# Attention and two gated layers: where conversions and projection groups stand around the ends of the attention chunks

## The chip, the cores and the metric

The kernel runs on one core of one Trainium2 chip. The metric is the device time of one execution in microseconds (us); less is better. Three executions of the kernel before took 965.5, 968.14 and 969.22 us, with a median of 968.14 us.

## What is computed

A causal attention with a window of 128 and a distance bias, then a gated layer (SiLU), then a second layer (Mish). Four sequences of 576 positions, eight heads of 64; its 2304 rows of 512 are the tokens of the two layers. Matrices arrive as 64-bit floats.

```python
# attention, per batch and head
scores = scale * np.matmul(q, k.transpose(0, 1, 3, 2))
mask = (rel >= 0) & (rel < window)
scores = np.where(mask, scores + bias[None], -1000000000.0)
attn = np.exp(scores - np.max(scores, axis=-1, keepdims=True))
attn = attn / (np.sum(attn, axis=-1, keepdims=True) + 1e-09)
out = np.matmul(attn, v)
...
# layer one, w_gate and w_val 512 x 1536, w_out 1536 x 512
g = x @ w_gate
silu = g * (1.0 / (1.0 + np.exp(-g)))
val = x @ w_val
x = silu * val @ w_out
...
# layer two, w_in 512 x 2048, w_out 2048 x 512
h = x @ w_in
sp = np.log1p(np.exp(h))
y = (h * np.tanh(sp)) @ w_out
```

## The kernel before

Numbers are kept as a high and a low part, and a product of two such numbers is three matmuls: high by high, high by low, low by high. `hi_act` makes the high part on ScalarE (line 121), `lo_dve` the low part on VectorE (line 124).

The 2304 tokens go in five chunks of 512, 384, 512, 512 and 384 (`A_CHUNKS`). Per chunk and head, the attention has these pieces. `score` multiplies on TensorE into a bank `s_ps`; VectorE adds bias and takes the maximum (line 233), ScalarE takes the exponential (line 237). `norm` takes a reciprocal on VectorE (line 248) and scales the probabilities on ScalarE (line 252) and, in chunk 0, partly on VectorE (line 254). `transp` transposes them on TensorE into `t_ps` (line 259), copies the bank to `PT` on ScalarE (line 265) and masks it twice on GpSimd (lines 268 and 272). `outp`, once for two heads, is the value product on TensorE into `o_ps`, whose high and low part become one quarter of `xt`, the input of layer one. Eight heads make four pairs and four quarters, 0 to 3.

Layer one of a chunk is a list of groups. For each of 12 columns of weights, `gv_groups` gives a gate group and a value group of 12 matmuls into `g_ps`, followed by ScalarE's tanh (line 628), VectorE's products (lines 629 and 637) and the parts `hh` and `hl`. `out_group` gives 12 matmuls of the output projection into four banks `acc0` to `acc3`. With a lag of one, the last output group of a chunk is carried into the next chunk's list. While a chunk's groups run, the next chunk's attention pieces are put between them: each piece has a cost, and is emitted when its share of the costs falls to the share of the groups that are done.

Weights are converted from 64-bit words on chip by `convert`: one pass on ScalarE (line 416, output `cg`) and four on VectorE (lines 428, 433, 421 and 439, outputs `cw` and `cp`), then `hi_act` and `lo_dve` into a tile `w` (layer one's gate and value weights, `conv_w1`) or `ring` (its output weights, `conv_ring`). The raw words come by DMA into `wst` and `wraw`, and the converted `ring` weights are also written to DRAM (`w1od`) for later chunks. All these steps wait in a queue `bg`, from which `pump` takes them. For the first attention `w` 0 and 1 and `ring` 0 are converted; the later ones are pumped during the groups of chunk 0. `begin` multiplies the first two columns by the quarters 0 and 1 of `xt`, and later by quarter 2, before the first attention is done.

The order of TensorE is that of the program (`manual_schedule`). The other engines' order is made by a scheduler with a timeline of its own, which may put a conversion ahead of attention work that comes earlier in the program. Each engine then works through its own order. DMAs are issued from the SP queue.

The main loop's emission of groups:

```python
for gi, (kind, i, f) in enumerate(groups):
    if ci == 0 and kind == "gv" and gi % 3 == 0:
        if i == 0:
            conv_ring(1)
        if i + 2 < NF1:
            conv_w1(i + 2)
    f()
    ...
    while win and (spent * ng < (gi + 1) * total or gi == len(groups) - 1):
        _, cost, e = win.popleft()
        e()
```

Of the kernel before, what the change touches and what calls it, by code (L numbers as in the profile page):

```python
# [18 lines left out]
B, H, S, D = 4, 8, 576, 64  # L19
# [3 lines left out]
NF1, NF2 = F1 // 128, F2 // 128  # L23
# [69 lines left out]
def body(ctx: ExitStack, tc: tile.TileContext, qT, kT, vP, w1, w1o, w2, cst, yT):  # L93
    nc = tc.nc
# [28 lines left out]
    def lo_dve(out, in_, hi):  # L123
        return nc.vector.tensor_tensor(out=out, in0=in_, in1=hi.bitcast(F32), op=ALU.subtract)  # L124
# [10 lines left out]
    def attention(ap, p, ci, s_native, upfront):  # L135
# [120 lines left out]
        def transp(h):  # L256
            t_ps = rot("t_ps")
            for q in sorted(p.qb, key=lambda q: -q.qn):
                nc.tensor.transpose(t_ps[:, q.c:q.c + q.qn], P_[h, q.idx][:q.qn], ident[:q.qn, :q.qn])  # L259
            pt = ap.tile([128, 2 * nb_, 128], F32, tag="PT", name="PT")  # L260
            pairs = pt.rearrange("p (u k) c -> p u k c", k=2)
            for u, m, n in p.runs:
                c = p.qb[u].c
                prev, here = pairs[:, u:u + m, 0, :n], pairs[:, u:u + m, 1, :n]
                nc.scalar.activation(  # L265
                    out=prev, in_=t_ps[:, c:c + m * n].rearrange("p (u c) -> p u c", u=m), func=AF.Copy
                )
                nc.gpsimd.affine_select(  # L268
                    out=here, in_=prev, pattern=[[0, m], [1, n]], compare_op=ALU.is_ge, fill=0.0,
                    base=0, channel_multiplier=-1,  # L270
                )
                nc.gpsimd.affine_select(
                    out=prev, in_=prev, pattern=[[0, m], [-1, n]], compare_op=ALU.is_gt, fill=0.0,
                    base=0, channel_multiplier=1,
                )
            pt_[h] = pt.rearrange("p s c -> p (s c)")

        def outp(pr):
            v = raw.pop(("v", pr))
            xt = x_t[ci]  # L280
            n = p.n
            o_ps = rot("o_ps")
            for i, x in enumerate(p.o_order):
                q, here = x.uses[0]
                c0, b0 = q.c, 256 * q.idx + 128 * here
                for e in range(2):
                    mm(
                        o_ps[64 * e:64 * e + 64, c0:c0 + x.w], v[:, x.vi, 64 * e:64 * e + 64],
                        pt_[2 * pr + e][:, b0:b0 + x.w], i == 0, False,
                    )  # L290
            hi_act(xt[:, 0, pr, :n], o_ps[:, :n])
            lo_dve(xt[:, 1, pr, :n], o_ps[:, :n], xt[:, 0, pr, :n])

        return SimpleNamespace(
            ci=ci, load=load, load_v=load_v, split=split, score=score, norm=norm, transp=transp,
            outp=outp, upfront=upfront, ns=len(p.sb), s_full=s_full, nk=len(p.kb),
        )

    early = {}

    def attention_pieces(atts):

# [55 lines left out]

        def t_piece(k):
            a, h = heads[k]  # L360
            return (a.ci, 0.48, lambda: a.transp(h))

        def delay(k):
            return CFG["delay0"] if heads[k][0].ci == 0 else 1
# [25 lines left out]
    def pump(n):  # L390
        while n > 0 and bg:
            k, f = bg.popleft()
            f()
            n -= 1
            if k is not None:
                done.add(k)
# [530 lines left out]
    with tc.manual_schedule(engines={mybir.EngineType.PE}):  # L927
# [28 lines left out]
        while at < lasts[0]:  # L956
# [10 lines left out]
            while bg and nst - len(bg) < f * nst:  # L967
                pump(1)
        carry = []
        for ci, p in enumerate(plansA):  # L970
            if ci < last:
                win = [pieces.popleft() for _ in range(lasts[ci + 1] - at)]
                at = lasts[ci + 1]
            else:
                pump(10000)
                att.__exit__(None, None, None)
                cv = tc.tile_pool(name="cv", bufs=2, side="right", reuse_waits="tile")
                bpool["p"] = cv.__enter__()
                win = []
                for b in range(NJ, NF2):  # L980
                    combos(b)
# [5 lines left out]
            if ci == last:  # L987
                first["x"] = load_x(xp, 0)
            groups = []
            outs = carry + [out_group(ci, i)[0] for i in range(NF1)]  # L990
            for i in range(NF1):
                groups += [("gv", i, f) for f in gv_groups(ci, i)]
                if i < len(carry) or len(outs) > NF1 - 1 - i + lag:
                    groups.append(("o", 0, outs.pop(0)))
            if ci == 0:
                groups[4:6] = groups[5], groups[4]
# [4 lines left out]
            win = collections.deque(win)  # L1001
            for gi, (kind, i, f) in enumerate(groups):
                if ci == 0 and kind == "gv" and gi % 3 == 0:
                    if i == 0:
                        conv_ring(1)
                    if i + 2 < NF1:
                        conv_w1(i + 2)
                f()
                if ci or not win:
                    pump(CFG["pump_g"])  # L1010
                elif gi % 3 == 0:
                    due = max(1, -(-len(bg) // 4))
                if not ci:
                    pump(due)
                while win and (spent * ng < (gi + 1) * total or gi == len(groups) - 1):
                    _, cost, e = win.popleft()
                    e()
                    spent += cost
                    pump(CFG["pump_p"] if ci else due)
# [76 lines left out]
```

## Time and profile before

| what | value |
|---|---|
| median of three executions | 968.14 us |
| the profiled execution | 969.0 us |
| its span, first to last instruction | 967.2 us |
| mean clock granted to TensorE | 0.994 of full |
| TensorE matmul busy | 924.9 us (96%) |
| TensorE weight loads busy | 828.4 us (86%) |
| VectorE busy | 701.2 us (72%) |
| ScalarE busy | 524.7 us (54%) |
| GpSimd busy | 193.8 us (20%) |

The page gives busy times over the whole span. A timeline row gives the start of an instruction (or of several alike), its duration, the engine, the line, what it writes and reads, and in brackets for how long the engine was idle before it and whose work ended that. In a row of a window, each engine's busy time is followed by its number of instructions, and PEclk is the clock granted to TensorE, 1.00 being 2.4 GHz and 0.50 being 1.2 GHz.

### The profile page before, as it was taken

To read this page: it belongs to the slowest core of one execution; us is meant where nothing else is said; L and a number is where in the kernel's file an instruction comes from. 1 tells how busy PE (TensorE), PEld (TensorE's weight loads), DVE (VectorE), ACT (ScalarE), POOL (GpSimd) and SP (SyncE) were. 2 spreads that over 40 slices of the span, in tenths; PEclk is the share of its full clock that TensorE was granted. 3 is DMA by queue.
4 is the path that set the end of the run, shared out by engine and by line. 5 is a ranking of instruction groups with operands and counts; after the bars stand their busy time and mean duration, and the time that the engine had idled before them with its cause. 6 is when DMAs were issued, how large, how long until landed. Compare 5 with 4: busy or idle time off the path is not lost.

```text
span 967.2 us, 14606 instructions
## 1 busy us (share of the span) xinstructions
PE 924.9 (96%) x5040; PEld 828.4 (86%) x5040; DVE 701.2 (72%) x1341; ACT 524.7 (54%) x1135; POOL 193.8 (20%) x332
## 2 busy tenths in 40 slices
PE   6879999999999999999999998799999999999998
PEld 4646777899988888887878998799999999999997
DVE  6989897688667865478434768778876888777673
ACT  6846666666666674455433445564544645455442
POOL 0321232111110222001103334442012320122000
PEclk9979999999999999999999999999999999999999
DMA  8865325386546733176306993624783257930375
GB/s 293 293 231 184 126 70 182 101 253 217 160 128 207 261 111 112 31 245 225 130 1 205 380 342 112 234 66 163 255 301 131 66 186 245 314 111 16 98 264 183
DMA packets 76921, 174.86 MB, mean 181 GB/s; under 512 B 9136, under 2 KB 52528, under 8 KB 67120
## 3 DMA queue, kind: packets, MB, share of 16 engines
q1 hardware_dynamic: 76848, 173.94, 54.0%
q8 instruction: 40, 0.66, 0.3%
q14 instruction: 33, 0.27, 0.1%
HBM read 138.25 MB, written 35.65 MB: 180 GB/s over the span
## 4 chain that ended last, share of the span: by engine, by line
PE 70%; DVE 10%; DMA 9%; ACT 4%; issue 3%; POOL 2%; SPq 2%; DVEq 0%; ACTq 0%; POOLq 0%
PE bk L114 29%; PE g_ps L114 24%; PE acc L114 11%; DMA wraw<-w 3%; PE s_ps L114 3%; PE o_ps L114 2%; DVE G L694 1%; DVE win L124 1%; POOL t L790 1%; DMA q<-qT 1%; PE t_ps L259 1%; DVE cw L433 1%; SPq L176 1%; DVE u L694 1%; DMA wout<-w2o 1%
## 5 line engine op out<-in xcount | busy, mean ns | idle before, releaser
L114 PE MATMUL g_ps<-xt,w 128*128 128x512 f32 (+1 forms) x1440 | 319.8, 375 | 5.1 <-DVE xt L124 3.8
L114 PEld LDWEIGHTS g_ps<-xt,w 128*128 128x128 f32 x1440 | 259.2, 189 | 42.5 <-DVE xt L124 5.0
L114 PE MATMUL bk<-xs,win 128*128 128x384 f32 x1008 | 179.1, 336 | 8.6 <-DVE G L694 6.0
L114 PEld LDWEIGHTS bk<-xs,win 128*128 128x128 f32 x1008 | 174.5, 188 | 12.7 <-DVE G L694 9.2
L114 PE MATMUL bk<-op,wout 128*128 128x384 f32 x1008 | 176.1, 334 | 1.7 <-DMA wout<-w2o 1.1
L114 PEld LDWEIGHTS bk<-op,wout 128*128 128x128 f32 x1008 | 174.7, 188 | 2.7 <-issue 1.8
L114 PE MATMUL acc<-hh,ring 128*128 128x512 f32 (+1 forms) x480 | 149.0, 373 | 1.7 <-DVE ring L124 1.7
L121 ACT ACTIVATE op<-G 128x768 fp32r<-128x768 f32 x84 | 70.8, 847 | 65.6 <-PE bk L114 63.1
L114 PEld LDWEIGHTS acc<-hh,ring 128*128 128x128 f32 x480 | 89.0, 188 | 14.6 <-DVE ring L124 2.3
L124 DVE TENSOR_TENSOR op<-G,op 128x768 fp32r<-128x768 f32 x84 | 80.3, 963 | 28.1 <-ACT op L121 27.4
L268 POOL TENSOR_SCALAR_AFFINE_SELECT PT<-PT 128x256 f32<-128x256 f32 (+4 forms) x80 | 44.5, 570 | 251.2 <-ACT PT L265 251.0
L114 PE MATMUL acc<-hl,ring 128*128 128x512 f32 (+1 forms) x240 | 88.6, 369 | 0.0
L790 POOL TENSOR_TENSOR t<-w 128x256 f32<-128x256 f32 x48 | 41.8, 891 | 230.3 <-DVE win L124 213.6
L237 ACT ACTIVATE Pt<-Pt,sm 128x128 f32<-128x128 f32 (+1 forms) x160 | 62.7, 395 | 16.2 <-DVE sm L233 15.5
L628 ACT ACTIVATE t<-g_ps 128x512 f32<-128x512 f32 (+1 forms) x60 | 32.9, 548 | 57.5 <-PE g_ps L114 57.4
L629 DVE SCALAR_TENSOR_TENSOR t<-t,g_ps 128x512 f32<-128x512 f32 (+1 forms) x60 | 37.7, 628 | 36.1 <-ACT t L628 36.0
L1040 ACT ACTIVATE G<-G 128x384 f32<-128x384 f32 x72 | 37.0, 521 | 49.2 <-DVE G L694 49.2
L694 DVE TENSOR_TENSOR G<-u,bk 128x384 f32<-128x384 f32 x72 | 39.0, 553 | 32.5 <-PE bk L114 30.3
L637 DVE SCALAR_TENSOR_TENSOR t<-t,g_ps 128x512 f32<-128x512 f32 (+1 forms) x60 | 37.9, 632 | 28.0 <-PE g_ps L114 26.7
L252 ACT ACTIVATE Pt<-Pt,sm 128x128 f32<-128x128 f32 (+1 forms) x144 | 46.5, 393 | 12.9 <-DVE sm L248 12.8
L121 ACT ACTIVATE hh<-t 128x512 fp32r<-128x512 f32 (+1 forms) x60 | 35.1, 585 | 32.9 <-DVE t L637 32.6
L124 DVE TENSOR_TENSOR hl<-t,hh 128x512 fp32r<-128x512 f32 (+1 forms) x60 | 40.6, 676 | 16.3 <-ACT hh L121 15.8
(78 smaller groups left out, 1240.5 us busy)
## 6 DMA issues: line engine op xcount, KB each, us to landing
wout<-w2o SPq DMA_DIRECT2D x42, 1024.0 KB, 6.3
wraw<-w SPq DMA_DIRECT2D x16, 1024.0 KB, 5.9
w2o<-chl SPq DMA_DIRECT2D x16, 896.0 KB, 8.9
wst<-w SPq DMA_DIRECT2D x12, 1024.0 KB, 7.9
cw<-w1od SPq DMA_DIRECT2D x24, 512.0 KB, 3.9
w<-w2d SPq DMA_DIRECT2D x24, 512.0 KB, 3.3
w2d<-cw SPq DMA_DIRECT2D x16, 512.0 KB, 4.6
wraw<-w1o SPq DMA_DIRECT2D x6, 1024.0 KB, 6.1
```

Of the source, the lines that this page charges most:

```text
L114: nc.tensor.matmul(out=out, lhsT=lhsT, rhs=rhs, start=start, stop=stop, skip_group_check=True)
L121: return nc.scalar.activation(out=out, in_=in_, func=AF.Copy)
L124: return nc.vector.tensor_tensor(out=out, in0=in_, in1=hi.bitcast(F32), op=ALU.subtract)
L237: nc.scalar.activation(out=Pt[:q.qn], in_=Pt[:q.qn], func=AF.Exp, scale=-1.0, bias=sm[:q.qn, i:i + 1], accum_out=sm[:q.qn, 8 + i:9 + i],)
L252: nc.scalar.activation(out=pt, in_=pt, func=AF.Copy, scale=r)
L268: nc.gpsimd.affine_select(out=here, in_=prev, pattern=[[0, m], [1, n]], compare_op=ALU.is_ge, fill=0.0, base=0, channel_multiplier=-1,)
L628: tanhs.append(nc.scalar.activation(out=t[:, :n], in_=st["g"][:, :n], func=AF.Tanh, scale=0.5))
L629: nc.vector.scalar_tensor_tensor(out=t[:, :n], in0=t[:, :n], scalar=1.0, in1=st["g"][:, :n], op0=ALU.add, op1=ALU.mult)
L637: nc.vector.scalar_tensor_tensor(out=t[:, :n], in0=t[:, :n], scalar=0.5, in1=vps[:, :n], op0=ALU.mult, op1=ALU.mult)
L694: nc.vector.tensor_tensor(out=out, in0=a, in1=b, op=op)
L790: nc.gpsimd.tensor_tensor(out=x[:, o], in0=a, in1=b, op=ALU.subtract)
L1040: nc.scalar.activation(out=out, in_=in_, func=AF.Mish)
```

## The change

Three things. First, while the groups of chunk 0 are emitted, each conversion step that `pump` takes is traced inside `issue_after`, which orders its instructions, on ScalarE behind the last copy to `PT` of the first attention, and on VectorE behind the low part of quarter 2 of `xt`; from chunk 1 on there is no such edge. Second, the cost of the last head's transposition is set from 0.48 to 3.08, and the output group that is carried over a chunk boundary goes to the head of the next chunk's list instead of behind its first two groups. Third, the first `conv_w1` in the loop goes ahead of `conv_ring(1)`.

```diff
--- before.py
+++ after.py
@@ -262,7 +262,7 @@
             for u, m, n in p.runs:
                 c = p.qb[u].c
                 prev, here = pairs[:, u:u + m, 0, :n], pairs[:, u:u + m, 1, :n]
-                nc.scalar.activation(
+                last_of["act"] = nc.scalar.activation(
                     out=prev, in_=t_ps[:, c:c + m * n].rearrange("p (u c) -> p u c", u=m), func=AF.Copy
                 )
                 nc.gpsimd.affine_select(
@@ -289,7 +289,7 @@
                         pt_[2 * pr + e][:, b0:b0 + x.w], i == 0, False,
                     )
             hi_act(xt[:, 0, pr, :n], o_ps[:, :n])
-            lo_dve(xt[:, 1, pr, :n], o_ps[:, :n], xt[:, 0, pr, :n])
+            last_of["x", pr] = lo_dve(xt[:, 1, pr, :n], o_ps[:, :n], xt[:, 0, pr, :n])
 
         return SimpleNamespace(
             ci=ci, load=load, load_v=load_v, split=split, score=score, norm=norm, transp=transp,
@@ -297,6 +297,8 @@
         )
 
     early = {}
+    last_of = {}
+    behind = []
 
     def attention_pieces(atts):
 
@@ -358,7 +360,7 @@
 
         def t_piece(k):
             a, h = heads[k]
-            return (a.ci, 0.48, lambda: a.transp(h))
+            return (a.ci, 0.48 + (2.6 if h == H - 1 else 0.0), lambda: a.transp(h))
 
         def delay(k):
             return CFG["delay0"] if heads[k][0].ci == 0 else 1
@@ -390,7 +392,10 @@
     def pump(n):
         while n > 0 and bg:
             k, f = bg.popleft()
-            f()
+            with ExitStack() as es:
+                for x in behind:
+                    es.enter_context(tc.issue_after(x.ins))
+                f()
             n -= 1
             if k is not None:
                 done.add(k)
@@ -967,7 +972,10 @@
             while bg and nst - len(bg) < f * nst:
                 pump(1)
         carry = []
+        behind += [last_of["act"], last_of["x", 2]]
         for ci, p in enumerate(plansA):
+            if ci:
+                behind.clear()
             if ci < last:
                 win = [pieces.popleft() for _ in range(lasts[ci + 1] - at)]
                 at = lasts[ci + 1]
@@ -987,10 +995,11 @@
             if ci == last:
                 first["x"] = load_x(xp, 0)
             groups = []
-            outs = carry + [out_group(ci, i)[0] for i in range(NF1)]
+            outs = [out_group(ci, i)[0] for i in range(NF1)]
+            groups += [("o", 0, f) for f in carry]
             for i in range(NF1):
                 groups += [("gv", i, f) for f in gv_groups(ci, i)]
-                if i < len(carry) or len(outs) > NF1 - 1 - i + lag:
+                if len(outs) > NF1 - 1 - i + lag:
                     groups.append(("o", 0, outs.pop(0)))
             if ci == 0:
                 groups[4:6] = groups[5], groups[4]
@@ -1001,10 +1010,10 @@
             win = collections.deque(win)
             for gi, (kind, i, f) in enumerate(groups):
                 if ci == 0 and kind == "gv" and gi % 3 == 0:
+                    if i + 2 < NF1:
+                        conv_w1(i + 2)
                     if i == 0:
                         conv_ring(1)
-                    if i + 2 < NF1:
-                        conv_w1(i + 2)
                 f()
                 if ci or not win:
                     pump(CFG["pump_g"])
```

What the scheduler and the program make of it, at three places. In these rows an `x3` counts rows alike, and the line numbers of the changed kernel are a few higher (428 is 433 there, 433 is 438, 421 is 426, 439 is 444, 629 is 634).

VectorE at the end of the first attention. Before, from the five passes ahead of quarter 2 of `xt` to quarter 3:

```order
L124 TENSOR_TENSOR w<-cw,w 128x1024
L428 TENSOR_SCALAR cw<-wst 128x1024 x2
L433 SCALAR_TENSOR_TENSOR cw<-wst,cw 128x1024 x2
L124 TENSOR_TENSOR xt<-o_ps,xt 128x512
L439 SCALAR_TENSOR_TENSOR cw<-cw,cp 128x1024
L421 TENSOR_SCALAR cp<-cg 128x512
L439 SCALAR_TENSOR_TENSOR cw<-cw,cp 128x1024
L124 TENSOR_TENSOR w<-cw,w 128x1024
L421 TENSOR_SCALAR cp<-cg 128x512
L428 TENSOR_SCALAR cw<-wraw 128x1024
L124 TENSOR_TENSOR w<-cw,w 128x1024
L124 TENSOR_TENSOR xt<-o_ps,xt 128x512
```

The same place in the change, from the last head's sums to quarter 3:

```order
L245 TENSOR_SCALAR sm<-sm 128x4
L248 RECIPROCAL sm<-sm 128x4
L254 TENSOR_SCALAR Pt<-Pt,sm 128x128 x2
L124 TENSOR_TENSOR xt<-o_ps,xt 128x512
L433 TENSOR_SCALAR cw<-wst 128x1024
L433 TENSOR_SCALAR cw<-wraw 128x1024
L438 SCALAR_TENSOR_TENSOR cw<-wst,cw 128x1024
L426 TENSOR_SCALAR cp<-cg 128x512
L438 SCALAR_TENSOR_TENSOR cw<-wraw,cw 128x1024
L444 SCALAR_TENSOR_TENSOR cw<-cw,cp 128x1024
L426 TENSOR_SCALAR cp<-cg 128x512
L124 TENSOR_TENSOR xt<-o_ps,xt 128x512
```

Before, five conversion passes stand ahead of quarter 2 of `xt`, and seven between it and quarter 3. In the change the sums, the reciprocal and the scaling of the last head are followed by quarter 2 at once, and the conversions begin behind it.

TensorE at the first transposition of chunk 1 (128x128 and 128x64, head 0). Before:

```order
L114 MATMUL acc_720<-hh,ring 128x512
L114 MATMUL acc_721<-hh,ring 128x512
L114 MATMUL acc_721<-hl,ring 128x512
L114 MATMUL acc_721<-hh,ring 128x512
L114 MATMUL g_ps<-xt,w 128x512 x12
L259 MATMUL t_ps<-cst_sb,Pt 128x128 x2
L259 MATMUL t_ps<-cst_sb,Pt 128x64 x2
L114 MATMUL s_ps<-k_634,q_633 128x256
```

In the change:

```order
L114 MATMUL acc_717<-hh,ring 128x512
L114 MATMUL acc_718<-hh,ring 128x512
L114 MATMUL acc_718<-hl,ring 128x512
L114 MATMUL acc_718<-hh,ring 128x512
L259 MATMUL t_ps<-cst_sb,Pt 128x128 x2
L259 MATMUL t_ps<-cst_sb,Pt 128x64 x2
L114 MATMUL g_ps<-xt,w 128x512 x12
L114 MATMUL s_ps<-k_634,q_633 128x256
```

The transposition has moved ahead of the 12 matmuls of a value group (`g_ps`), and stands directly behind an output group.

TensorE at the end of the last attention, that of chunk 4, during the groups of chunk 3. Before:

```order
L114 MATMUL acc_4614<-hl,ring 128x512
L114 MATMUL acc_4614<-hh,ring 128x512
L259 MATMUL t_ps<-cst_sb,Pt 128x128 x3
L114 MATMUL o_ps<-PT,v 64x256 x2
L114 MATMUL o_ps<-PT,v 64x128 x4
L114 MATMUL o_ps<-PT,v 64x256 x2
L114 MATMUL g_ps<-xt,w 128x512 x24
```

In the change the last two transpositions come first:

```order
L114 MATMUL g_ps<-xt,w 128x512 x12
L259 MATMUL t_ps<-cst_sb,Pt 128x128 x3
L114 MATMUL g_ps<-xt,w 128x512 x12
L259 MATMUL t_ps<-cst_sb,Pt 128x128 x3
L114 MATMUL acc_4611<-hh,ring 128x512
L114 MATMUL acc_4611<-hl,ring 128x512
```

and, after further groups of both kinds, the last value product:

```order
L114 MATMUL acc_4614<-hl,ring 128x512
L114 MATMUL acc_4614<-hh,ring 128x512
L114 MATMUL g_ps<-xt,w 128x512 x12
L114 MATMUL o_ps<-PT,v 64x256 x2
L114 MATMUL o_ps<-PT,v 64x128 x4
L114 MATMUL o_ps<-PT,v 64x256 x2
L114 MATMUL g_ps<-xt,w 128x512 x12
```

Before, the value product (`o_ps`) directly follows the last transposition. In the change three gate or value groups of 12 and two output groups stand between them, and one more gate or value group follows the value product.

## Rows read from the trace of the kernel before

**Rows 1.** The page's slices: clock granted to TensorE, tenths, 40 slices.

```profile
PEclk9979999999999999999999999999999999999999
```

**Rows 2.** Timeline, TensorE, 39 to 67 (start us, us, engine line op, idle before <- releaser).

```profile
39.06 1.81 PE L114 MATMUL s_ps<-qkv 64*128 64x256 f32 x8
...
42.06 0.66 PE L259 MATMUL t_ps<-cst_sb,Pt 128*128 128x128 f32 x4 [1.18 <-ACT PT L265]
...
44.44 4.85 PE L114 MATMUL g_ps<-xt,w 128*128 128x512 f32 x20 [0.79 <-DVE xt L124]
...
49.22 1.74 PE L114 MATMUL o_ps<-PT,qkv 128*64 128x256 f32 x16
...
50.89 0.81 PE L259 MATMUL t_ps<-cst_sb,Pt 128*128 128x128 f32 x4
...
54.78 1.19 PE L259 MATMUL t_ps<-cst_sb,Pt 128*128 128x128 f32 x4 [3.09 <-ACT Pt L252]
...
59.18 5.06 PE L114 MATMUL g_ps<-xt,w 128*128 128x512 f32 x11 [2.77 <-DVE xt L124]
...
64.17 1.92 PE L114 MATMUL o_ps<-PT,qkv 128*64 128x256 f32 x16
...
66.79 0.49 PE L114 MATMUL g_ps<-xt,w 128*128 128x512 f32 x1 [0.70 <-ACT xt L121]
```

**Rows 3.** Timeline, ScalarE, at 53.

```profile
53.33 1.11 ACT L416 ACTIVATE cg<-wraw 128x1024 bf16<-128x1024 bf16 x1 [2.23 <-DMA wraw<-w1o]
```

**Rows 4.** Timeline, VectorE, 54 to 67.

```profile
54.52 1.29 DVE L428 TENSOR_SCALAR cw<-wst 128x1024 int32<-128x1024 int32 x2 [2.75 <-DMA w1od<-cw]
...
58.45 0.68 DVE L124 TENSOR_TENSOR xt<-o_ps,xt 128x512 fp32r<-128x512 f32 x1
...
66.77 0.69 DVE L124 TENSOR_TENSOR xt<-o_ps,xt 128x512 fp32r<-128x512 f32 x1 [0.84 <-ACT xt L121]
```

**Rows 5.** Windows of 1 us (window, then us, busy and count per engine, PEclk, DMA).

```profile
54.00:55.00 1.00, 0.22 (x1) 0.18 (x1) 0.48 (x1) 1.00 (x4) 0.00 (x0) 0.68 1.04 442
...
64.00:65.00 1.00, 1.00 (x7) 0.58 (x8) 1.00 (x3) 0.00 (x0) 0.00 (x0) 0.70 0.00 0
```

**Rows 6.** Timeline, TensorE and VectorE, 80 to 85.

```profile
80.57 2.91 PE L114 MATMUL g_ps<-xt,w 128*128 128x512 f32 x12
...
84.41 0.89 PE L259 MATMUL t_ps<-cst_sb,Pt 128*128 128x128 f32 x4 [0.94 <-ACT Pt L252]
...
82.39 0.16 DVE L248 RECIPROCAL sm<-sm 128x4 f32<-128x4 f32 x1
```

**Rows 7.** Windows, two long stretches.

```profile
67.50:162.00 94.50, 91.53 (x451) 68.83 (x452) 87.29 (x199) 61.01 (x163) 21.57 (x43) 1.00 0.43 140
...
10.00:50.00 40.00, 35.18 (x146) 25.47 (x144) 39.62 (x136) 34.35 (x101) 11.23 (x18) 1.00 0.87 301
```

**Rows 8.** Timeline, GpSimd, masks of PT.

```profile
34.13 0.64 POOL L268 TENSOR_SCALAR_AFFINE_SELECT PT<-PT 128x512 f32<-128x512 f32 x1 [0.77 <-ACT PT L265]
...
58.98 2.21 POOL L272 TENSOR_SCALAR_AFFINE_SELECT PT<-PT 128x512 f32<-128x512 f32 x2
```

**Rows 9.** Timeline, TensorE, 505 to 511.

```profile
505.64 0.49 PE L259 MATMUL t_ps<-cst_sb,Pt 128*128 128x128 f32 x3
...
509.18 1.51 PE L114 MATMUL o_ps<-PT,v 128*64 128x256 f32 x14 [2.48 <-POOL PT L272]
```

**Rows 10.** Groups of instructions by line, VectorE conversion passes (count | busy, mean ns).

```profile
L439 DVE SCALAR_TENSOR_TENSOR cw<-cw,cp 128x1024 f32<-128x1024 f32 x34 | 42.5, 1249 | 0.2
...
L421 DVE TENSOR_SCALAR cp<-cg 128x512 int32<-128x512 int32 x34 | 15.2, 448 | 8.6 <-ACT cg L416 8.5
...
L428 DVE TENSOR_SCALAR cw<-wraw 128x1024 int32<-128x1024 int32 x22 | 15.8, 718 | 11.8 <-DMA wraw<-w 5.6 <-DMA x2d<-ev 2.7 <-DMA v<-vP 2.6
```

**Rows 11.** Timeline, VectorE, 182 to 184.

```profile
182.51 0.69 DVE L637 SCALAR_TENSOR_TENSOR t<-t,g_ps 128x512 f32<-128x512 f32 x1 [0.48 <-PE g_ps L114]
...
183.97 0.69 DVE L124 TENSOR_TENSOR hl<-t,hh 128x512 fp32r<-128x512 f32 x1 [0.77 <-ACT hh L121]
```

## The prediction

> **What bounds the kernel now.** I read the slices of the page first: the clock row of TensorE, which is busy for 96% of the span, has one dent, the third slice, from 48 to 73 us [rows 1]. The reader should see that this is the only place before the second layer where much time is lost. The TensorE timeline then names the losses in order [rows 2]. Head 6's transposition stands at 50.89; head 7's waits 3.09 us for ScalarE's normalisation; the matmuls on the third pair of attention outputs wait 2.77 us for VectorE's `xt`; after the last value product come 0.70 us. The queues of the other two engines say why. ScalarE stood 2.23 us at a conversion's first pass, `cg<-wraw`, whose DMA had not landed, with head 7's normalisation behind it [rows 3]. VectorE stood 2.75 us at a conversion that waited for a spill, and ran four conversion passes ahead of `xt` at 58.45 [rows 4]. The clock went to half during the first wait (0.68 in the microsecond from 54, 0.70 in that from 64 on its way back) [rows 5]: eleven matmuls took 5.06 us there, and twelve of the same kind take 2.91 at full clock [rows 2, 6]. From then on VectorE is the engine with least room: it is busy 87.29 of the 94.5 us from 67.5 to 162, and 39.62 of 40 in the stretch ahead [rows 7].
>
> **Part one: the tail of the first attention.** Twenty-one conversion passes that stood on VectorE between 37 us and the last `xt` become seven, and those stand behind the third `xt`; on ScalarE the passes go behind the last copy to `PT`. So nothing of a conversion can block the tail. I time the tail anew from 39.06, with the durations of before. Scores end at 40.87; the next transposition no longer waits 1.18 us for a `PT` copy that a conversion held up, nor the 24 matmuls behind it 0.79 [rows 2]: 49.22 becomes 47.3. Value product 1.67 (49.22 to 50.89) gives 49.0; two transpositions of some 0.7 give 50.4, as head 7's normalisation has no conversion in front. Twelve matmuls of 0.25 follow (20 took 4.85), to 53.4. GpSimd's masks are next: in the trace they end at 61.19, 5.22 us after head 7's transposition ended at 55.97 [rows 2, 8], so here at 55.6; TensorE waits 2.2 us. Value product 1.92 gives 57.5. From its end to the end of the last `xt` took 1.37 (66.09 to 67.46) [rows 2, 4], so 58.9 against 67.46: **8.6 us ahead**. Bounds: 10.8, if each mask takes the 0.64 of the row at 34.13 and not the 1.1 of those at 58.98 [rows 8], for TensorE then waits for nothing; 6.6 if the 2.0 us before 49.22 are not had.
>
> **What is late next.** The changed order puts head 0's transposition of the second chunk one group of twelve matmuls (2.91 us) earlier on TensorE, while on VectorE the reciprocal that it needs has two more 1.25 us passes (a `ring` and a `w`) between it and the last `xt`. Before, that reciprocal came 14.9 us after `xt` (82.39 less 67.46) [rows 4, 6]; with 2.3 more it comes at 58.9 + 17.2 = 76.1. The transposition followed 2.0 us later; the exponentials of head 1 that stood between are done by then, so I take 1.0: 77.1. TensorE would arrive at 83.47 - 67.46 - 2.9 after `xt`, that is 72.0, and waits 5.1 us where it waited 0.94 [rows 6]. Transposition and the twelve matmuls behind it end at 77.1 + 0.9 + 2.9 = 80.9; the same work was done at 85.3. So 4.4 of the 8.6 stay, **minus 4.2**. Bounds: nothing lost, if the passes fit into gaps; 6.2, if the 2.0 stays and the spill of the ring is waited for again.
>
> The clock is the next price. A wait of 3.09 us let it fall [rows 2, 5]; one of 2.48 us near 507 did not, since the slices there show 9 [rows 1, 9]. A wait of 5.1 is on the far side of the first. At half clock twelve matmuls cost about 2.6 more (5.06 for eleven against 2.91). While TensorE is slow VectorE works off its passes, which it would have had to be waited for anyway, so I take half, **minus 1.3**, between 0 (the row at 507) and 2.6. The Trainium skill (TensorE: Matmul & The Clock Gate, HAM oscillation — how this bites in real kernels) says that a wait in the middle of a kernel puts the array back to its low clock, so that what follows each one starts slow; by it this term is the full 2.6 and the forecast 1.3 later, and the trace agrees at 54 us but not at 507.
>
> Then the backlog. To the tenth product of a tanh with its gate, eleven more conversion passes stand behind the last `xt` than did: six long ones near 1.25, three of 0.45, two of 0.72 [rows 10], together 9.4 us when the 0.08 by which rows overlap is taken off. VectorE thus has 87.3 + 9.4, some 97 us of work from 58.9 on, where it got to 162 before. At a density of 0.97 that is 158.9, 3.1 us ahead; this is what the three terms leave (8.6 - 4.2 - 1.3), so they need 0.97, less than the 0.99 before 50 us and more than the 0.924 after it [rows 7]. I count nothing more for it, and keep 0.924 (163.9, 1.9 behind) for the range. The loads that move with the conversions are hidden: the SP queue holds the same ones, later, and their readers are later by as much.
>
> **Part two: the chunk boundaries.** Before the last chunk the last transposition (505.64) stands directly ahead of the last value product, which waits 2.48 us for its mask [rows 9]. The changed order has three groups of twelve gate or value matmuls and two of the output projection between them, far over the 2.5: **plus 2.5**. The other three boundaries have other heads' scores there and no such wait. The output projection that was carried into the next chunk now follows the one before it directly, so its operands, `hh` and `hl`, have to be ready in 2.8 us instead of after two groups more. At 182.51 the chain from VectorE's product to the end of `hl` takes 2.15 us [rows 11], so it mostly fits; I put **minus 0.4** for four boundaries, between 0 and 2. The swap of the first two conversions goes together with part one. The second layer's order on TensorE is unchanged, and costs nothing.
>
> **Sum:** 8.6 - 4.2 - 1.3 + 2.5 - 0.4 = 5.2. The profiled execution took 969.0, so 963.8; the median of the three runs lies 0.9 lower, and on its scale I forecast **962.9**.
>
> **Rivals.** *The tail's gain is kept*: masks run unblocked (10.8) and the clock stays: 10.8 - 4.2 + 2.5 - 0.0 = 9.1, or 959.0 on the median's scale; with the transposition's wait half gone, 957. For it speaks that a mask took 0.64 in places; against it that conversions now start just when the masks run.
>
> *All of the tail's gain is given back*: the wait at the transposition is the full 6.2 and the clock costs 2.6, so that only 2.1 from the boundaries is left: 966. This is also the case that part one does not do what it says, the wait only moving from one transposition to another.
>
> *Slower*: VectorE's backlog becomes the bound of the whole first chunk. The place is its queue from 58.9 to the tenth group, the price 97 us over its density. Below 0.922 the loss there passes the 2.1 of the boundaries, and the kernel is slower than before; at 0.86 the queue gets there at 171.7, 9.7 late, and the time is 975.7. For it: VectorE takes its order as it stands, whatever DMA or ScalarE pass it waits for, as at 54.52 [rows 4], and it showed 0.924 in this stretch [rows 7]; against: it had TensorE to wait for there, and 0.99 when it had work. The Trainium skill (Perfetto Trace Analysis, Identifying the Most-Contended Engine) takes the engine with the highest occupancy for the one to relieve and warns that a busy TensorE row is no measure; by it VectorE decides in this chunk, as in this rival, while the trace shows TensorE without waits there.
>
> **How the numbers follow.** The forecast case has 0.50, with 960 to 966 as its own range; the kept gain 0.22, the gain given back 0.18, the backlog 0.10. A measurement of this kernel can tell about 0.5% from no change, that is 963.3 and 973.0. A little over half of the forecast case (0.27) lies below 963.3, with all of the kept gain: faster 0.49. The rest of it (0.23), the given-back case and the mild end of the backlog (0.03): same 0.44. Slower 0.07. The range from 956 to 970 takes in the bounds of the terms and leaves out about 1 in 10 at either end.
>
> **What would show it.** Right: both waits of 3.09 and 2.77 gone, no DMA wait on ScalarE or VectorE between 50 and 56, the last `xt` of the first chunk done near 59; a wait of 4 to 6 us at the first transposition after it, perhaps with the clock at half; VectorE near 0.97 from 59 to 159; no mask wait near 505. Wrong: a last `xt` after 62, a new wait for `hl` over half a microsecond at the boundaries, or new TensorE waits in the second layer.

## The result and the profile after

The changed kernel takes 979.66 us in the median (four runs, 977.14 to 981.91) where the kernel before, run beside it, takes 968.68: 1.0126 of its time, 95% interval 1.0089 to 1.0163. It is about 11 to 12 us slower; faster was forecast. The profiled execution took 978.84 us, its span is 977.1, and TensorE's mean clock 0.991 of full. Of the executions behind the numbers below, two (one of the kernel before, 1028.64 us, and one with the carried group first, 1289.37 us) ran at a clock of 0.85 and 0.66; they stand in no ratio and move no median by more than 0.3 us.

The clock row of the page, against [rows 1], has its first dent in the fourth slice instead of the third, and TensorE's busy row has an 8 in the ninth and the eleventh slice (195 to 220 and 244 to 269 us), where it had 9 before:

```profile
PE   5988999989899999999999999989999999999998
...
PEclk9998999999999999999999999999999999999999
```

The tail of the first attention ended when it was forecast to. These rows of the timeline answer to [rows 2, 4]: the waits of 3.09 and 2.77 us are gone, the value product waits 0.73 for its mask, and the last `xt` ends at 58.98.

```profile
49.29 1.09 PE L259 MATMUL t_ps<-cst_sb,Pt 128*128 128x128 f32 x8
51.25 2.80 PE L114 MATMUL g_ps<-xt,w 128*128 128x512 f32 x11 [0.23 <-DVE xt L124]
...
55.36 1.73 PE L114 MATMUL o_ps<-PT,qkv 128*64 128x256 f32 x14 [0.73 <-POOL PT L272]
...
76.60 1.17 PE L259 MATMUL t_ps<-cst_sb,Pt 128*128 128x128 f32 x4 [4.50 <-ACT Pt L252]
77.70 5.36 PE L114 MATMUL g_ps<-xt,w 128*128 128x512 f32 x12
...
58.30 0.68 DVE L124 TENSOR_TENSOR xt<-o_ps,xt 128x512 fp32r<-128x512 f32 x1
```

The transposition at 76.60 is that of head 0 of the next chunk, where a wait of 5.1 us was forecast; the clock is at its lower level (0.50) behind it, as these windows of 4 us show, and the twelve matmuls that follow take 5.36 us:

```profile
72.00:76.00 4.00, 0.09 (x1) 0.00 (x0) 4.00 (x16) 2.80 (x10) 0.00 (x0) 0.99 0.89 283
76.00:80.00 4.00, 3.40 (x10) 2.47 (x10) 4.00 (x7) 4.00 (x11) 2.49 (x2) 0.50 0.66 277
80.00:84.00 4.00, 4.00 (x12) 2.46 (x10) 3.19 (x6) 0.95 (x4) 3.73 (x7) 0.65 0.94 337
```

To see where the time is lost, compare the two kernels at places where TensorE has done exactly the same matmuls, though not in the same order. That is so at the start of each of these three pairs of rows, which lie near the beginning of chunks 1, 2 and 3. First the three rows before, then the three after:

```profile
193.34 0.60 PE L259 MATMUL t_ps<-cst_sb,Pt 128*128 128x128 f32 x4
...
291.47 0.76 PE L259 MATMUL t_ps<-cst_sb,Pt 128*128 128x128 f32 x5
...
411.09 0.28 PE L114 MATMUL s_ps<-K,Q 128*128 128x256 f32 x1
```
```profile
191.29 0.60 PE L259 MATMUL t_ps<-cst_sb,Pt 128*128 128x128 f32 x4
...
301.70 0.76 PE L259 MATMUL t_ps<-cst_sb,Pt 128*128 128x128 f32 x5
...
424.37 0.28 PE L114 MATMUL s_ps<-K,Q 128*128 128x256 f32 x1
```

The changed kernel is 2.05 us ahead at the first place, 10.23 behind at the second and 13.28 at the third. Some 12 us are lost in chunk 1, which has 384 tokens, and 3 more in chunk 2. Nothing more is lost later on balance. Below, "on the same work" stands for this comparison.

TensorE's timeline in chunk 1 has three long waits there that it did not have (before, none is over 0.65 us); the last row is the last boundary:

```profile
198.64 0.44 PE L114 MATMUL acc<-hl,ring 128*128 128x384 f32 x1 [1.44 <-DVE hl L124]
...
222.00 0.39 PE L114 MATMUL s_ps<-K,Q 128*128 128x256 f32 x1 [3.70 <-DVE Q L193]
...
249.47 0.39 PE L114 MATMUL s_ps<-K,Q 128*128 128x256 f32 x1 [2.82 <-DVE Q L193]
...
531.16 0.50 PE L114 MATMUL acc<-hl,ring 128*128 128x512 f32 x1 [1.43 <-DVE hl L124]
```

So it is VectorE that is late, with the low part of `Q` for the next head's scores. VectorE's own queue tells what it did in the meantime:

```profile
190.44 0.69 DVE L433 TENSOR_SCALAR cw<-wraw 128x1024 int32<-128x1024 int32 x1
...
192.62 1.23 DVE L438 SCALAR_TENSOR_TENSOR cw<-wraw,cw 128x1024 f32<-128x1024 uint32 x1
...
194.27 0.54 DVE L642 SCALAR_TENSOR_TENSOR t<-t,g_ps 128x384 f32<-128x384 f32 x1
194.74 1.38 DVE L124 TENSOR_TENSOR ring<-cw,ring 128x1024 fp32r<-128x1024 f32 x1
196.04 1.21 DVE L444 SCALAR_TENSOR_TENSOR cw<-cw,cp 128x1024 f32<-128x1024 f32 x1
...
198.04 0.55 DVE L124 TENSOR_TENSOR hl<-t,hh 128x384 fp32r<-128x384 f32 x1
...
207.46 0.69 DVE L433 TENSOR_SCALAR cw<-wraw 128x1024 int32<-128x1024 int32 x1 [5.04 <-DMA wraw<-w]
...
216.24 1.23 DVE L438 SCALAR_TENSOR_TENSOR cw<-wraw,cw 128x1024 f32<-128x1024 uint32 x1
```

Two things stand there. The `hl` that TensorE wants at 197.2 comes behind two long passes of conversions (1.38 and 1.21). And from 202.4 VectorE stands 5.04 us at the first pass of a conversion of layer two's weights (`conv_w2`), whose raw words have not landed, and everything of the attention and the groups stands behind it in its order. From there the conversions follow one another as fast as their one raw tile allows. The SP queue issues the load of the next raw words at 209.95, 217.53 and 224.98, each within 0.1 us of the pass that reads the old ones last (that of 216.24 ends at 217.47):

```profile
197.81 0.43 SPq L475 DMA_DIRECT2D wraw<-w  x1
209.95 0.33 SPq L475 DMA_DIRECT2D wraw<-w  x1
217.53 0.33 SPq L475 DMA_DIRECT2D wraw<-w  x1
224.98 0.34 SPq L475 DMA_DIRECT2D wraw<-w  x1
236.01 0.33 SPq L475 DMA_DIRECT2D wraw<-w  x1
```

Five loads within 38.2 us, the second to the sixth of the sixteen of layer two; before, the same five take 73.8 us, of which these are the first and the last:

```profile
166.31 0.43 SPq L470 DMA_DIRECT2D wraw<-w  x1
...
240.11 0.44 SPq L470 DMA_DIRECT2D wraw<-w  x1
```

### The profile page after: what moved, and what is told of

Its sections match the earlier page's. It is cut to its first block, busy times and chain, and to the rows that moved or that the text cites. A ratio compares the mean times of both kernels' runs of the same rounds, so it can differ in the third digit from the quotient of the medians.

```text
span 977.1 us, 14620 instructions
## 1 busy us (share of the span) xinstructions
PE 929.4 (95%) x5040; PEld 833.5 (85%) x5040; DVE 701.8 (72%) x1341; ACT 526.0 (54%) x1135; POOL 202.2 (21%) x332
## 5 line engine op out<-in xcount | busy, mean ns | idle before, releaser
L268 POOL TENSOR_SCALAR_AFFINE_SELECT PT<-PT 128x256 f32<-128x256 f32 (+4 forms) x80 | 47.7, 612 | 238.2 <-ACT PT L265 238.1
L795 POOL TENSOR_TENSOR t<-w 128x256 f32<-128x256 f32 x48 | 44.0, 936 | 225.9 <-DVE win L124 206.1
L114 PEld LDWEIGHTS acc<-hl,ring 128*128 128x128 f32 x240 | 46.3, 193 | 8.4 <-DVE hl L124 3.5
```

What stands on the lines that cost most here:

```text
L114: nc.tensor.matmul(out=out, lhsT=lhsT, rhs=rhs, start=start, stop=stop, skip_group_check=True)
L268: nc.gpsimd.affine_select(out=here, in_=prev, pattern=[[0, m], [1, n]], compare_op=ALU.is_ge, fill=0.0, base=0, channel_multiplier=-1,)
L795: nc.gpsimd.tensor_tensor(out=x[:, o], in0=a, in1=b, op=ALU.subtract)
```

## The experiments

Two theories at first. *B*: the boundary part does it, by its effect on the order inside chunk 1. *C*: the conversions that part one moved late into chunk 0 push layer two's back, and with them VectorE's work of chunk 1. The edits of the change can be made apart. All ratios are to the kernel before, run on the same chip, with their 95% intervals; unless an edit is shown the kernel is the changed one.

**Part one alone.** Cost and carried group are as before:

```diff
-            return (a.ci, 0.48 + (2.6 if h == H - 1 else 0.0), lambda: a.transp(h))
+            return (a.ci, 0.48, lambda: a.transp(h))
-            outs = [out_group(ci, i)[0] for i in range(NF1)]
-            groups += [("o", 0, f) for f in carry]
+            outs = carry + [out_group(ci, i)[0] for i in range(NF1)]
-                if len(outs) > NF1 - 1 - i + lag:
+                if i < len(carry) or len(outs) > NF1 - 1 - i + lag:
```

> Only the conversions of the first chunk are ordered behind the tail (and the two converters swapped); the costs of the pieces and the place of the carried output group are as before, so TensorE's order is that of before. Theory B (the boundary part brings chunk 1's attention pieces onto TensorE ahead of VectorE's splits): the tail's gain of about 4.4 us at the end of chunk 0 is kept and the loss is gone, 963 to 966, ratio 0.995. Theory C (the conversions moved late into chunk 0 push the layer-two conversions and with them VectorE's work of chunk 1 back): chunk 1 still loses about 12 us, 975 to 981, ratio 1.01.

Measured: 962.86 us, 0.9966 (0.9939 to 0.9993). Theory C falls: the moved conversions alone do no harm.

**The boundary part alone**, without the ordering behind the tail and with the two converters as before:

```diff
-        behind += [last_of["act"], last_of["x", 2]]
```

> Only the boundary part: the dearer last transposition and the carried output group first; the conversions of the first chunk are as before. Theory B: the loss of chunks 1 and 2 stays and the tail's gain is missing, 980 to 986, ratio 1.012 to 1.018. Theory C: the wait of 2.48 us at the last boundary goes and nothing else, 965 to 969, ratio 0.997 to 1.000.

Measured: 982.98 us, 1.0175 (1.0123 to 1.0227). So the boundary part costs about 15 us alone (17 by the ratio), and 16.8 on top of part one (979.66 less 962.86; 15.5 by the ratios).

This run also tells what the long stand at 202.4 is worth. In chunk 1 VectorE's order is that of the changed kernel, row for row (128 instructions from the first conversion on), but the load lands sooner: VectorE stands 1.00 us at the same pass instead of 5.04. TensorE waits for `Q` all the same:

```profile
209.91 0.69 DVE L433 TENSOR_SCALAR cw<-wraw 128x1024 int32<-128x1024 int32 x1 [1.00 <-DMA wraw<-w]
...
225.31 0.39 PE L114 MATMUL s_ps<-K,Q 128*128 128x256 f32 x1 [1.73 <-DVE Q L193]
...
252.67 0.58 PE L114 MATMUL s_ps<-K,Q 128*128 128x256 f32 x1 [3.53 <-DVE Q L193]
```

On the same work this kernel is 4.4 us behind before chunk 1 and 14.6 behind after it. It loses 10.2 us there, where the changed kernel loses 12.3. So, as far as these two executions tell, the late load is some 2 us of the loss, and most of it comes without it.

**Its two edits apart, each with part one.** First the cost without the carried group's new place (of the diff for part one, all but its first pair of lines), then the new place without the cost (the first pair alone):

> As changed, but the carried output group stands behind the first two groups of the chunk again. If the dearer last transposition (which makes every other piece of a chunk's window come later against the groups or earlier, as their shares of the total change) is what costs: about 976 to 982, a wait of TensorE for Q of 2 us or more in 215 to 255. If the carried group's place is: 962 to 967 and no such wait.

> As changed, but every transposition costs 0.48 again; the carried output group is first in the chunk. If the carried group's place is what costs: about 976 to 982 with waits for Q of 2 us or more in 215 to 255. If the dearer transposition is: 962 to 967 and no such wait. If each has a share: about 970 for both this kernel and the one with the cost kept.

Measured: 964.59 us with the cost, 0.9975 (0.9944 to 1.0005), which cannot be told from part one alone; 971.6 us with the carried group first, 1.0043 (1.0012 to 1.0074). So the carried group's place is the larger edit: it costs 8.7 us by itself. The dearer transposition costs at most some 2 alone (1.7 by the medians) but 8.1 more where the carried group stands first. On the same work in chunk 1 they lose 1.4 and 7.7 us apart, and 12.3 together.

The waits did not come quite as expected. With the cost alone there is a wait for `Q` of 2.30 us at 238.52, though the time is that of part one. With the carried group first none for `Q` is over 0.56 us in 215 to 255; TensorE waits there for other things, at most 1.66 us for `hh`. So a wait for `Q` is one form of the loss and not the only one. Its five loads take 36.1 us (196.36 to 232.46), as tight as in the changed kernel: a lump of this size cost 7.7 us in chunk 1 with the pieces at their old costs, and 12.3 with the dearer transposition.

How? TensorE's orders, printed one against the other, show it. In part one's order chunk 1 begins with the first two groups, the carried output group, two more groups, an output group. In the changed order two output groups stand back to back, and then come four groups with two heads' scores and no output group for 11 us. An output group gives VectorE no new work (it reads `hh` and `hl`, which were made for it before); a gate or value group asks for a product and perhaps a low part, a head's scores for a split and a maximum. From this two theories of the mechanism. *D*: VectorE's conversions of layer two now come in a lump into that stretch, and behind their loads the splits are late. *E*: TensorE's order by itself does it.

**The conversions spread out.** From chunk 1 on one background step instead of two is taken behind each group and each piece; TensorE's order is the changed one, row for row. The five loads now take 49.6 us (196.59 to 246.17).

```diff
-                    pump(CFG["pump_g"])
+                    pump(1 if ci else CFG["pump_g"])
-                    pump(CFG["pump_p"] if ci else due)
+                    pump(1 if ci else due)
```

> The changed kernel, with one background step instead of two behind each group and each piece from chunk 1 on, so that the five conversions of the second layer's weights spread over chunk 1 instead of standing in its first 45 us; TensorE's order is that of the changed kernel, row for row. Theory D (the boundary part drops the first output group out of the first 11 us of chunk 1, so that the passes of the conversions come to VectorE in a lump, hold the splits of Q behind their loads, and TensorE waits): most of the 17 us against part one alone comes back, 963 to 969, no wait for Q over 1.5 us between 205 and 260. Theory E (TensorE's own order does it: two output groups back to back, then four groups and two heads' scores with nothing in between that spares VectorE): the time stays at 975 to 981 and the waits for Q stay.

Measured: 967.81 us, 0.9991 (0.9970 to 1.0012): 12 of the 17 us come back with the same TensorE order. The waits of VectorE that the profile puts down to DMAs add up to 6.1 us in chunk 1, against 6.2 in the changed kernel, so it is not their sum that differs. Between 205 and 260 one wait for `Q` of 1.96 us is left, over the 1.5 that D named, and the wait of 1.44 for `hl` is still there:

```profile
197.52 0.44 PE L114 MATMUL acc<-hl,ring 128*128 128x384 f32 x1 [1.44 <-DVE hl L124]
...
239.67 0.39 PE L114 MATMUL s_ps<-K,Q 128*128 128x256 f32 x1 [1.96 <-DVE Q L193]
```

**No conversions of layer two in chunk 1**; the sixteen lie in chunks 2 and 3.

```diff
-            if 1 <= ci < last:
-                k = last - 1
-                for i in range((ci - 1) * NF2 // k, ci * NF2 // k):
+            if 2 <= ci < last:
+                k = last - 2
+                for i in range((ci - 2) * NF2 // k, (ci - 1) * NF2 // k):
```

> The changed kernel with the five conversions of chunk 1 taken out of it: the sixteen conversions lie in chunks 2 and 3, eight each. TensorE's order is that of the changed kernel. Theory D: chunk 1's loss of about 12 us goes (end of chunk 1, by the first copy of its accumulators, near 282 instead of 293.5), chunks 2 and 3 lose up to 5 each more, 966 to 975 in all. Theory E: the end of chunk 1 stays at 290 or later and the time at 976 to 984.

Measured: 970.97 us, 1.0015 (0.9993 to 1.0037). Chunk 1 ends at 278.79 (VectorE's first copy of its accumulators, `ev<-acc`), 14.7 us earlier than in the changed kernel (293.48), and the loss reappears where the conversions went, in chunk 2:

```profile
327.24 1.75 PE L114 MATMUL o_ps<-PT,v 128*64 128x256 f32 x24 [2.31 <-DVE s_ps L226]
...
351.33 0.58 PE L114 MATMUL s_ps<-K,Q 128*128 128x256 f32 x1 [3.17 <-DVE Q L193]
```

The stretch from 185 to 295 us sums it up, by windows: the second number is TensorE's busy time out of 110, the fourth VectorE's, PEclk comes before the last two. First before, then the changed kernel, part one alone, the conversions spread, and none in chunk 1:

```profile
185.00:295.00 110.00, 108.46 (x681) 101.80 (x681) 80.83 (x208) 70.49 (x193) 17.95 (x38) 1.00 0.58 176
```
```profile
185.00:295.00 110.00, 100.06 (x621) 95.04 (x620) 73.48 (x188) 64.79 (x168) 13.40 (x24) 0.97 0.53 166
```
```profile
185.00:295.00 110.00, 109.12 (x676) 101.08 (x676) 83.11 (x213) 71.74 (x197) 17.28 (x39) 1.00 0.57 183
```
```profile
185.00:295.00 110.00, 106.12 (x672) 100.27 (x670) 80.99 (x208) 70.97 (x191) 17.56 (x36) 1.00 0.58 183
```
```profile
185.00:295.00 110.00, 109.85 (x695) 103.59 (x694) 69.72 (x199) 66.92 (x188) 20.33 (x40) 1.00 0.40 115
```

TensorE stands 9.9 us in the changed kernel and runs slower for part of the rest (0.97), but 3.9 with the conversions spread and 0.2 without them. VectorE is less busy in the changed kernel only because less of the work falls into the window (621 matmuls for 681). For the same work, that between the places named above, it is busy 73.24 us of 110.4 in the changed kernel (191.3 to 301.7) and 73.72 of 98.0 in part one alone (187.7 to 285.7). It does the same work, later. Of theory D the runs thus bear out the conversions in this TensorE order; the waits behind their loads are the smaller part, as the boundary part alone showed.

**Is a lump enough by itself?** Part one alone with TensorE's order of before, and four background steps in chunk 1:

```diff
-                    pump(CFG["pump_g"])
+                    pump(4 if ci == 1 else CFG["pump_g"])
-                    pump(CFG["pump_p"] if ci else due)
+                    pump((4 if ci == 1 else CFG["pump_p"]) if ci else due)
```

> Part one alone, with four background steps instead of two behind each group and piece of chunk 1, so that the conversions there are asked for earlier; TensorE's order is that of before. Theory D in its plain form (a lump of conversions in chunk 1 is enough, whatever TensorE's order): 967 to 976, waits for Q of 2 us or more in 190 to 260. If the lump hurts only where TensorE's order has the scores early and no output group near: 961 to 966, ratio under 0.998.

Measured: 962.86 us, 0.9943 (0.9912 to 0.9973). This does not decide as cleanly as meant: the scheduler put the third and fourth load earlier (172.66 and 184.91 for 196.41 and 205.75), so the five take 49.0 us and the lump was a smaller one. A wait for `Q` of 2.85 us appeared at 217.45 and chunk 1 lost some 2.4 us on the same work, where part one lost none, but the whole lost nothing. Whether a full lump does harm in TensorE's order of before stays open.

**Does spreading help where nothing is lumped?** Part one alone with one background step:

> Part one alone, with one background step instead of two behind each group and piece from chunk 1 on; TensorE's order is that of before. Theory D: little to gain, since TensorE waits under 1 us for Q in chunk 1 there: 960 to 964. Theory E: the same. If slower by 3 us or more, the spread conversions cost by themselves (for the ring tiles that the output groups wait for), and the run with the changed kernel's order has to be read with that.

Measured: 964.95 us, 0.9959 (0.9937 to 0.9981). It gains nothing there, so what it gives the changed order is no general gain of fewer steps. It even has a wait for `Q` of 2.67 us at 216.09, where part one has none over 0.3 in chunk 1.

**The boundary part where its wait is.** Part one, the dearer transposition for the very last head alone, and the carried group where it was:

```diff
-            return (a.ci, 0.48 + (2.6 if h == H - 1 else 0.0), lambda: a.transp(h))
+            return (a.ci, 0.48 + (2.6 if k == n - 1 else 0.0), lambda: a.transp(h))
```

> Part one, with the dearer transposition for the very last head alone (chunk 4's, at the boundary from chunk 3) and the carried output group where it was: the wait of 2.47 us for the masked tile at that boundary goes and no other chunk's pieces move. 2 to 3 us under part one alone: 959 to 961, ratio 0.990 to 0.994. If the pieces of that last window, moved by the dearer one, make waits of their own: 963 or more.

Measured: 960.2 us, 0.9921 (0.9897 to 0.9944), the fastest median of all and faster than both kernels. The value product at the last boundary, which waits 2.47 us in part one alone, as in [rows 9], no longer waits:

```profile
505.63 1.52 PE L114 MATMUL o_ps<-PT,v 128*64 128x256 f32 x16
```

**The swap of the converters** taken back in that kernel:

```diff
+                    if i == 0:
+                        conv_ring(1)
                     if i + 2 < NF1:
                         conv_w1(i + 2)
-                    if i == 0:
-                        conv_ring(1)
```

> As the fastest so far (part one, and the dearer transposition for the very last head alone), with the two converters in the order of before (the second output tile ahead of the gate tile). If the ordering behind the tail does all of part one's work: 959 to 962, the same as with the swap. If the swap is needed, since the output tile's passes stand ahead of the gate tile's that the first groups wait for: 963 to 968.

Measured: 961.65 us, 0.9929 (0.9894 to 0.9964). The swap makes no difference that can be told; the ordering behind the tail is all of part one.

## Why the prediction was wrong, step by step

*The tail* (8.6 us ahead): right in its mechanism, and exact in part by luck. The last `xt` was forecast at 58.9 and ends at 58.98. The wait for the masks was 0.73 us instead of 2.2; the matmuls ahead of it ended some 0.6 later than forecast, and from the end of the value product to the end of `xt` it took 1.89 instead of 1.37.

*What is late next* (minus 4.2): right in its mechanism in the changed kernel, where the transposition waits 4.50 us for a forecast of 5.1. With TensorE's order of before the same wait is 1.72, with the carried group first and no dearer transposition 1.87, with the dearer one alone 4.50: it is the earlier place of the transposition, which comes with the cost, that makes it long.

*The clock* (minus 1.3): it fell behind this wait, to the lower level between 76 and 80. The twelve matmuls behind it took 5.36 us instead of 2.91, so the term measured about 2.5, nearly the upper bound: the half that was put down to VectorE working off its passes was not had. On the same work the lead falls by 6.3 us at this place, from 8.5 (75.67 before, 67.19 after) to 2.2 (85.21 and 82.99), where the two terms had 5.5. The Trainium skill's rule cited there (TensorE: Matmul & The Clock Gate, HAM oscillation — how this bites in real kernels) is meant for long waits, and is borne out by this one and by that of 3.70 us in chunk 1, after which the window 220 to 230 shows 0.83. The wait of 2.48 us near 507, behind which the clock stayed, is thus no case against it, as the prediction took it to be. But the clock fell behind shorter waits too: 2.82 us (0.83 in the window 250 to 260), and 1.72 in part one alone (last section). There the measurement decides.

*The backlog* (nothing more): right. VectorE is busy 95.83 of the 100 us from 59 to 159, a density of 0.96 for the forecast 0.97. The lead at the end of chunk 0 is 2.05 us where the three terms left 3.1; the clock makes most of the difference. The rival of a slower kernel through this backlog is not what happened; its chunk and its cause were others, and the occupancy by which the Trainium skill (Perfetto Trace Analysis, Identifying the Most-Contended Engine) would find it does not show it: for the same work in the stretch that loses 12 us VectorE is busy 73.24 of 110.4 us, and 73.72 of 98.0 in part one alone, which loses nothing there. Part one alone measures 968.16 x (1 - 0.9966) = 3.3 us by its ratio and 5.3 by the medians. It cannot be held against the 3.1, since the long wait at the transposition comes with the cost and not with part one.

*The last boundary* (plus 2.5): right where it stands alone. The wait is gone, and the medians differ by 2.7.

*The other three boundaries* (minus 0.4 for all four, between 0 and 2): this is the step that failed. In its place the changed kernel loses 12.3 us in chunk 1 and 3.1 in chunk 2 on the same work, where the sum had next to nothing. I asked only whether `hl` would be ready for the second of two output groups. At the first three boundaries it is; at the last the group waits 1.43 us, inside the bound. What I left out is VectorE's other work behind the boundary. The carried output group had stood between the first two pairs of gate and value groups, where it gave VectorE nothing new to do. Without it the first output group of chunk 1 itself waits 1.44 us at 198.64, the conversions of layer two fall into one lump, and the scores wait for `Q`. The sentence that these boundaries have "no such wait" looked at the waits that were there, for masks, and not at those that the new order would make. Of the dearer last transposition the sum held only its first effect, the earlier transposition in chunk 0. It also raises the total of every chunk's costs and so brings all its other pieces earlier; for that there was no term, and with the carried group first the cost comes to 8.1 us in all. The whole boundary part measures minus 16.8 on top of part one, some 3.6 of them in chunk 0 on the same work (2.05 ahead instead of 5.6).

*What would make it wrong*: the sign named there, a new wait for `hl` over half a microsecond at the boundaries, did appear; but the larger waits were for `Q`.

What is shown and what is argued: that the boundary part costs, that the carried group's place is the larger edit, and that conversions of layer two in this TensorE order carry about 12 of the 17 us are shown by the runs. That the late load is the smaller part of it is shown by the boundary part alone. How the rest comes about in detail (passes of conversions ahead of `Q`, `hl` and the products in VectorE's order) is read from the rows and not shown by a run of its own. Why the scheduler packs the conversions there is not shown either. It may be that four groups in a row take background steps of which no output group claims any for reloading its weights. What the traces do show is where the lump begins: the second load of layer two is issued between 160 and 171 us, before chunk 1, in every kernel with the carried group behind, and between 196 and 205 in those with it first that convert in chunk 1. The 4.9 us by which the spread version (967.81) stays behind part one alone were not taken apart by a run; on the same work 2.5 of them are lost in chunk 0, where the transposition waits 4.77 us. The waits for `hl` that are left, 1.44 us at 197.52 among them, are part of the rest. More raw tiles, which would let the loads run ahead of VectorE, were not tried.

## What to carry to other kernels

When a group of matmuls is moved, ask not only whether its own operands are ready but what it covered where it stood: a group that gives the busy vector engine no new work can be breathing space for it. VectorE works through one order here, and was late for everything behind a background pass, whether the pass waited for its load (5.04 us) or hardly did (1.00). So background work has to be paced by the work that stands behind it, and an edit to a shared cost or list has to be read in every chunk that uses it, not only at the wait it was made for. Apply such an edit only at the one place where the profile shows the wait.

## What the hardware showed unexpectedly

The length of a wait did not settle whether TensorE's clock fell. In part one alone the transposition's wait of 1.72 us at 75.18 was followed by 0.68 from 76 to 80; in the version with four background steps the same wait, 1.76 us, with nearly the same work ahead of it, was followed by full clock:

```profile
72.00:76.00 4.00, 2.28 (x12) 1.39 (x10) 4.00 (x12) 3.94 (x14) 0.10 (x1) 1.00 0.94 381
76.00:80.00 4.00, 4.00 (x14) 2.77 (x13) 4.00 (x9) 3.20 (x8) 3.16 (x1) 0.68 0.28 117
```
```profile
72.00:76.00 4.00, 2.24 (x12) 1.36 (x10) 4.00 (x12) 3.95 (x14) 0.11 (x1) 1.00 0.93 385
76.00:80.00 4.00, 4.00 (x19) 2.86 (x18) 4.00 (x9) 3.19 (x8) 3.16 (x1) 1.00 0.27 115
```

And one load of a megabyte took far longer than its kind: issued at 197.81, its first readers, on ScalarE and VectorE, started at 207.46, 9.6 us later, where the median to landing of these loads is 6.2 in the same profile.
